# A linear-attention kernel on one core: the scores of a step made two steps ahead, its small products in two halves, and a new order

## The chip, the core and the metric

The kernel runs on one core of one Trainium2 chip. TensorE (PE) multiplies, with its weight loads overlapping the products; VectorE (DVE), ScalarE (ACT) and GpSimd (POOL) do the element work; SyncE (SP) issues nearly all loads. What is measured is the device time of one execution in microseconds.

## The reference

Attention with a decaying state feeds a gated feed-forward block. Inputs are q, k, v of shape (4, 8, 768, 64), `w_in` (512, 1024), `conv_w` (3, 1024) and `w_out` (1024, 512). Cut to what is computed:

```python
state = zeros((B, H, D, D))
for t in range(S):
    state = gamma[None, :, None, None] * state + einsum('bhd,bhe->bhde', k[:, :, t], v[:, :, t])
    y[:, :, t] = scale * einsum('bhd,bhde->bhe', q[:, :, t], state)
x = y.transpose(0, 2, 1, 3).reshape(B, S, H * D)
h = maximum(x @ w_in, 0)
conv_out[t] = conv_w[0] * h[t-1] + conv_w[1] * h[t] + conv_w[2] * h[t+1]     # per channel
out = (h * sigmoid(conv_out)) @ w_out
```

## The kernel before, in words

**Steps.** Tokens are taken in chunks of 64, for two of the four batches at a time, so there are 24 steps: 0 to 11 for the first two batches, 12 to 23 for the others. A step `n` holds all 8 heads of its chunk. The recurrence is done per chunk: scores (k times q, 64x64 for each head and batch), masked with the decay by VectorE (`masked`, L823), then multiplied with v ("within" the chunk); q times the state that earlier chunks left ("across"), where the state is copied out of PSUM by ScalarE (`carry`, L831, tile `cy`); and the update of the state in PSUM (tile `ps_st`). Steps 0 and 1 have a wider form of their own. q is scaled by VectorE first (`scale_q`, L716), v by VectorE (L722) or ScalarE (L741).

**The small products.** All of these are issued by `multiply` (L772). `mix(n)` issues those of a step, two by two in turn from two lists: 32 scores of step n+1 beside 32 "within" products of step n in records of the trace, then 32 updates of the state beside 32 "across" products. A product of the scores or of the state goes from one half of the array's rows to the same half of its columns, a product of y to the other half, so the two lists in turn use all four quarters of the array. Step 2 makes its own scores (`EARLY = 2`); a list without a partner stands alone (`mix.23` has neither next scores nor a state to update).

**The large products.** y is copied out (`y_copy`, L859, from unit 1 on) and turned into x by `x_head` (ScalarE, L909) and `x_rest`, `xt_rest` (VectorE, through `difference`, L855). Four steps make a unit, six units in all. Unit 0 multiplies x with `w_in` plainly (`mm1`, L1022, 12 records a product); units 1 to 5 by a seven-product scheme on halves and sums of the operands (`fast`, L1022, 6 records). Sums of these in SBUF (`hc`, L1054, L1049), the convolution (`conv_tap` L1089 on ScalarE, `conv_side` L1094 on VectorE), the gate (L1099, L1104) and a split of the result in two (`g_head` L1112, `g_rest` L1121) lead to the second product with `w_out` (`mm2`, L1246, 6 records; `seven` L1223 in the last unit), and `put` (L1250) copies the output to SBUF for its store.

**What sets the order.** The order on each engine is written out by hand as one string of letters per engine (`ORDER`, L80), and each engine runs its string strictly in turn. `list_tasks` (L192) names each task's dependencies; `plan` (L409) walks the strings once, at build time, and decides which of the buffers of a pool a task takes (`BUFS`: 4 `rw` buffers, one per step in flight, each holding q, k, kt and v; 7 PSUM banks `ps`; one `cy`). On the chip a task waits for its data and for the last user of its buffer. The loads stand on SyncE's queue in the order of the `DMA` string, at most 8 in flight (`fetch`, L617 to L626), so a load that waits for its buffer holds up the loads behind it.

The string of TensorE is read like this: `a` is a `mix`, `A` to `C` are `mm1` and `fast` of the units 0 and 1, `o` and `O` are `mm2` and later letters further units, `u` is `seven`. The lines that the prediction speaks of are those named above; in the changed file they stand 16 to 23 lines lower (L772 becomes L788, L823 L846, L716 L732, L855 L878, L1022 L1045, L1246 L1269).

Of the kernel before, what the change touches and what calls it, by code (L numbers as in the profile page):

```python
# [29 lines left out]
NC = S // C  # L30
# [44 lines left out]
EARLY, V_ON_ACT = 2, [*range(WIDE, 8), *range(14, N_STEPS)]  # L75
# [6 lines left out]
        "rfsfrgqssatataAAqAAAaaABBBBBaBAABBaaaooCCCIOICCCIOOICCCOIOoIoCOooCCIooIooOooOaoooaooooooooaooooooooDDDJa"  # L82
        "JDDDJPPJDDDJPPaJDPPPDDJaJoPoooaooaoooooooooEEEKoKEEEKQQKEQQQEEKaKEEEKoKQQQaooaooaooooooooFFFLoLoFFFLRRLF"
        "RRRFFLaLFFFLRoLRoRaaooooooGGGMoMoSSGGGMoMoSSoGGGMoMoSSoGGGMoMoSSuuuuuuuuuuuuuuuuuuuuuuuuuuuuuuuuuuuuuuuu"
        "uuuuuuuuuuuuuuuu"
    ),
    "DVE": (
        "kmtkqtmmmmbrbqrllb9blmlbqqlr0b9mBlr9b80mqq0ybzylzbbmdlq9ellvyqrrm332244r3m2j4r3j2j46j8ymzzb0IdCCyyObIeCC"
        "lOzzIbldCvClbqeOvyybbzzldlClyeIyzzOydmyqzzyzyedqqCmzveyyzzdvred3r322rr44e332244mjjjjqhmqvDDJPDDyyJzzPmyD"
        "zJPDyzJddeDqDyzyPzmrqerrm3d3y3224eyzz6rdj424e324mjjj8qqEiEQKEEyKQqyKzzmyyzzdEdEEeQQKreqmyEyzzmrr33y232d4"  # L90
        "y4rzz234e2jj64dj8mejhiFFhLRqFLFyyzRLzymyqzzFddReFyFyLzzmrr332244FeRrr332244djjjjiehyGGyMSzzyyzziGGdMSday"
        "eyfGzzMSGedyaeyzGzfMSGdayyzzefdaefuuuuuuuuuuuuuu"
    ),
# [60 lines left out]
def states_with(n):  # L154
    if n == NC:
        return []
    return [NC] if n == NC - 1 else [n] * (n % NC + 1 < NC)
# [251 lines left out]
def plan(tasks):  # L409
# [17 lines left out]
    def earliest(k):  # L427
# [13 lines left out]
        for name, _ in take:  # L441
            if len(slots[name]) < sum(name == x for x, _ in take):
                return None
# [920 lines left out]
```

## Time and profile before

| what | value |
|---|---|
| median of three runs | 333.06 us (331.17 to 334.36) |
| the profiled execution, its own time | 333.49 us |
| its span, first to last instruction | 331.7 us |
| PE busy | 319.0 us, 96% of the span |
| VectorE busy | 290.2 us, 88% |
| ScalarE busy | 221.6 us, 67% |
| granted TensorE clock | 1.00 throughout |
| the chain that ended last | PE 82%, DVE 6%, DMA 5%, ACT 3%, issue 2% |

A row of the timeline gives the start, the duration, the engine, the line, what is written and read, the shapes and the number of instructions put together; in brackets stands how long the engine was idle just before, and what ended that. "issue" there means a wait for nothing that the profile shows. Durations of PE overlap their neighbours a little, since matmuls are pipelined: the time that a group takes is the distance from its start to the next group's start. The span is 1.8 us shorter than the execution's own time, and the execution itself 0.43 us above the median.

### The profile page before, as it was taken

To read this page: it belongs to the slowest core of one execution; us is meant where nothing else is said; L and a number is where in the kernel's file an instruction comes from. 1 tells how busy PE (TensorE), PEld (TensorE's weight loads), DVE (VectorE), ACT (ScalarE), POOL (GpSimd) and SP (SyncE) were. 2 spreads that over 40 slices of the span, in tenths; PEclk is the share of its full clock that TensorE was granted. 3 is DMA by queue.
4 is the path that set the end of the run, shared out by engine and by line. 5 is a ranking of instruction groups with operands and counts; after the bars stand their busy time and mean duration, and the time that the engine had idled before them with its cause. 6 is when DMAs were issued, how large, how long until landed. Compare 5 with 4: busy or idle time off the path is not lost.

```text
span 331.7 us, 10665 instructions
## 1 busy us (share of the span) xinstructions
PE 319.0 (96%) x4551; PEld 286.6 (86%) x4551; DVE 290.2 (88%) x551; ACT 221.6 (67%) x447; POOL 25.8 (8%) x64
## 2 busy tenths in 40 slices
PE   7998998899999999999999999999999999999995
PEld 5787998799878888999788999888999979899994
DVE  1999899899999979679999088999789999999976
ACT  1687898886668655389867466986537773767630
POOL 2000000000101011100000100002010013001100
PEclk9999999999999999999999999999999999999999
DMA  7996954792004541522256203260001001001103
GB/s 241 388 358 219 344 182 143 243 393 98 0 3 131 158 121 73 208 81 68 94 171 214 76 21 99 78 213 0 3 33 37 2 34 63 0 3 63 65 0 128
DMA packets 21019, 40.21 MB, mean 121 GB/s; under 512 B 2742, under 2 KB 3254, under 8 KB 20972
## 3 DMA queue, kind: packets, MB, share of 16 engines
q1 hardware_dynamic: 19228, 34.15, 30.4%
q0 software_dynamic: 1600, 5.24, 4.1%
q8 instruction: 36, 0.59, 0.7%
q10 hardware_dynamic: 144, 0.13, 0.1%
q14 instruction: 11, 0.09, 0.1%
HBM read 33.23 MB, written 6.29 MB: 119 GB/s over the span
## 4 chain that ended last, share of the span: by engine, by line
PE 82%; DVE 6%; DMA 5%; ACT 3%; issue 2%; SPq 1%; DVEq 0%; ACTq 0%
PE ps L1022 35%; PE ps L1246 31%; PE ps L772 7%; PE ps L1223 6%; PE ps_st L772 4%; DMA w<-in_w_in 3%; DMA rw<-in_qk 2%; SPq L624 1%; DVE g L1121 1%; DVE hc L1054 1%; DVE t L855 1%; DVE hc L1094 1%; DVE hc L1104 1%; DVE xa L855 0%; DVE rw L823 0%
## 5 line engine op out<-in xcount | busy, mean ns | idle before, releaser
L1246 PE MATMUL ps<-w,g 128*128 128x512 f32 x480 | 118.1, 397 | 0.0
L1246 PEld LDWEIGHTS ps<-w,g 128*128 128x128 f32 x480 | 87.7, 188 | 19.0
L1022 PE MATMUL ps<-xa,w 128*128 128x256 f32 (+3 forms) x552 | 76.4, 283 | 0.5 <-DVE rw L823 0.4
L1022 PEld LDWEIGHTS ps<-xa,w 128*128 128x128 f32 x552 | 70.7, 189 | 2.6 <-ACT w L990 0.6
L1022 PE MATMUL ps<-xa,s 128*128 128x256 f32 (+2 forms) x480 | 69.3, 282 | 0.0
L1094 DVE SCALAR_TENSOR_TENSOR hc<-hc,cw_sb,hc 128x512 f32<-128x512 f32 (+1 forms) x96 | 68.1, 743 | 1.3 <-ACT hc L1089 1.2
L1022 PEld LDWEIGHTS ps<-xa,s 128*128 128x128 f32 x480 | 62.5, 189 | 1.8 <-ACT hc L1049 0.2
L1054 DVE CUSTOM_DVE_ANT_0 hc<-ps,hc 128x256 f32<-128x256 f32 (+2 forms) x80 | 32.5, 419 | 16.1 <-ACT hc L1049 10.4
L1049 ACT COPY hc<-ps 128x256 f32<-128x256 f32 (+2 forms) x60 | 22.2, 372 | 35.1 <-PE ps L1022 33.0
L1089 ACT ACTIVATE hc<-hc,cw_sb 128x512 f32<-128x512 f32 x48 | 33.5, 722 | 11.8 <-DVE hc L1054 8.5
L772 PEld LDWEIGHTS ps<-rw 64*64 64x64 f32 (+2 forms) x1472 | 27.8, 136 | 8.5 <-ACT t L859 2.1
L772 PE MATMUL ps<-rw 64*64 64x64 f32 (+2 forms) x1472 | 31.6, 223 | 2.9 <-ACT t L859 1.9
L1099 ACT ACTIVATE hc<-hc 128x1024 f32<-128x1024 f32 x24 | 25.2, 1060 | 7.9 <-DVE hc L1094 7.8
L1104 DVE TENSOR_TENSOR hc<-hc,hc 128x1024 f32<-128x1024 f32 x24 | 29.1, 1217 | 1.1 <-ACT hc L1099 1.0
L855 DVE TENSOR_TENSOR xa<-t,xa 128x384 fp32r<-128x384 f32 (+5 forms) x45 | 24.7, 567 | 3.7 <-ACT xa L909 1.2
L772 PE MATMUL ps<-rw,cy 64*64 64x64 f32 x672 | 24.3, 219 | 1.9 <-issue 1.9
L772 PE MATMUL ps_st<-rw 64*64 64x64 f32 (+1 forms) x672 | 24.4, 219 | 1.2 <-issue 1.0
L1121 DVE TENSOR_TENSOR g<-hc,g 128x1024 fp32r<-128x1024 f32 x20 | 24.4, 1220 | 1.3 <-ACT g L1112 1.3
L1112 ACT CAST g<-hc 128x1024 fp32r<-128x1024 f32 x20 | 21.0, 1049 | 5.8 <-PE ps L1246 3.7
L772 PEld LDWEIGHTS ps<-rw,cy 64*64 64x64 f32 x672 | 21.8, 135 | 2.2 <-issue 2.2
L772 PEld LDWEIGHTS ps_st<-rw 64*64 64x64 f32 (+1 forms) x672 | 22.0, 135 | 1.6 <-issue 1.2
L741 ACT ACTIVATE rw<-rw,const_sb 128x128 f32<-128x128 f32 x64 | 20.5, 395 | 0.0
(89 smaller groups left out, 356.2 us busy)
## 6 DMA issues: line engine op xcount, KB each, us to landing
rw<-in_qk SPq DMA_DIRECT2D x48, 256.0 KB, 3.6
rw<-in_kv SPq DMA_DIRECT2D x46, 256.0 KB, 4.4
out_y<-t POOLq DMA_DIRECT2D x20, 256.0 KB, 2.3
w<-in_w_in SPq DMA_DIRECT2D x16, 256.0 KB, 5.2
w<-in_w_out SPq DMA_DIRECT2D x16, 256.0 KB, 5.3
out_y<-t SPq DMA_DIRECT2D x2, 256.0 KB, 2.0
out_y<-t SPq DMA_DIRECT2D x3, 128.0 KB, 1.7
out_y<-t ACTq DMA_DIRECT2D x1, 128.0 KB, 1.8
```

Of the source, the lines that this page charges most:

```text
L772: nc.tensor.matmul(out, lhsT, rhs, start=start, stop=stop, skip_group_check=True)
L855: nc.vector.tensor_tensor(out=out, in0=in0, in1=in1, op=ALU.subtract)
L1022: nc.tensor.matmul(ps, w(a, k), x(b, k), start=first and i == 0, stop=last, skip_group_check=True)
L1049: nc.scalar.copy(quarter(u, p, *((0, 1), (0, 0), (1, 1))[i]), strip("X", u, p))
L1054: nc.vector._custom_dve(dve_ops.TENSOR_ADD_SAT, out=quarter(u, p, *out), in0=strip(bank, u, p), in1=quarter(u, p, *other), s0=float("inf") ...
L1089: nc.scalar.activation(cv, h, AF.Copy, scale=w)
L1094: nc.vector.scalar_tensor_tensor(out=cv, in0=h, scalar=w, in1=cv, op0=ALU.mult, op1=ALU.add)
L1099: nc.scalar.activation(cv, cv, AF.Sigmoid)
L1104: nc.vector.tensor_tensor(out=cv, in0=h, in1=cv, op=ALU.mult)
L1112: nc.scalar.copy(g_of(u, p)[:, 0], cv_of(u, 2 * p))
L1121: nc.vector.tensor_tensor(out=lo, in0=cv_of(u, 2 * p), in1=hi.bitcast(F32), op=ALU.subtract)
L1246: nc.tensor.matmul(ps, g, w, start=(f == 0 and i == 0), stop=(f == NF - 1 and i == 2))
```

## The change

`mix(n)` is cut in two tasks, `half(n)` and `mix(n)`. Each runs one pair of lists: the "within" products of step n beside scores, or the "across" products beside the update of the state. Normally "within" comes first; in the steps of `ACROSS_FIRST` (10, 15, 17, 19, 22) it comes second. The scores that stand beside the "within" products are those of step n+1 up to step 7, and from step 8 on those of step n+2 (`TWO_AHEAD = 8`). Step 9 lies at the border: nobody makes its scores ahead, so `scores.9` is a task of its own (`OWN`). Step 22 has no scores to stand beside its "within" products any more. `halves(n)` says what a step's halves hold:

```diff
-EARLY, V_ON_ACT = 2, [*range(WIDE, 8), *range(14, N_STEPS)]
+OWN, TWO_AHEAD, ACROSS_FIRST = (0, 1, 2, 9), 8, (10, 15, 17, 19, 22)
+V_ON_ACT = [*range(WIDE, 8), *range(14, N_STEPS)]
...
+def halves(n):
+    state = n + 1 if n == NC - 1 else n if n % NC + 1 < NC and n != NC else None
+    scored = n + 1 + (n >= TWO_AHEAD)
+    within = ("within", scored if scored < N_STEPS else None)
+    if n % NC == 0:
+        return [within]
+    return [("across", state), within] if n in ACROSS_FIRST else [within, ("across", state)]
...
+    def run_half(n, i):
+        kind, extra = halves(n)[i]
+        across, straight = list(of_y(n, kind)), []
+        if extra is not None:
+            straight = list(of_scores(extra) if kind == "within" else of_state(extra))
+        for at in range(0, len(across), 2):
+            for product in straight[at : at + 2] + across[at : at + 2]:
+                multiply(*product)
+
+    @emits
+    def half(n):
+        run_half(n, 0)
...
-        across = list(of_y(n))
-        straight = list(of_scores(n + 1)) if EARLY < n + 1 < N_STEPS else []
-        straight += [product for m in states_with(n) for product in of_state(m)]
-        for i in range(0, max(len(across), len(straight)), 2):
-            for product in straight[i : i + 2] + across[i : i + 2]:
-                multiply(*product)
+        run_half(n, len(halves(n)) - 1)
```

The dependencies in `list_tasks` follow (a `masked` after the half that made its scores, a `carry` after the "across" half), and `plan` may now give one task two banks of the same pool. All five order strings are new. The number of products is the same, and so is the number of tasks on VectorE, ScalarE, POOL and of the loads. The start of TensorE's string, where `h` is a half and `s` a `scores`:

```diff
-        "rfsfrgqssatataAAqAAAaaABBBBBaBAABBaaaooCCCIOICCCIOOICCCOIOoIoCOooCCIooIooOooOaoooaooooooooaooooooooDDDJa"
+        "rrsfsgqfsaatthqaAAAAAhaAhaABBBhaBBBBABhahaohasoCCCIOICCCIOOICCCOOIooIooCooOoooCoCIooIohaOoOhooahaooooooo"
```

Three places in the new order.

On TensorE, at the end of step 7 and the start of step 8. Before, the last "across" pairs of step 7 (`rw_3` and `cy_0` are its buffers) are followed at once by step 8, whose "within" products (into `ps_1_1146`) stand beside the scores of step 9 (`rw_1` into `ps_3_1147`):

```order
L772 MATMUL ps_st_83<-rw_3_572 64x64 x2
L772 MATMUL ps_3_1060<-rw_3_572,cy_0_1053 64x64 x2
L772 MATMUL ps_3_1147<-rw_1_882 64x64 x2
L772 MATMUL ps_1_1146<-rw_0_726 64x64 x2
L772 MATMUL ps_3_1147<-rw_1_882 64x64 x2
```

After, one large product `mm2` stands between, the scores beside step 8 (into `ps_5_1165`) are those of step 10, whose buffer `rw_2` is the one that step 6 used:

```order
L788 MATMUL ps_st_83<-rw_3_589 64x64 x2
L788 MATMUL ps_5_1062<-rw_3_589,cy_0_1099 64x64 x2
L1269 MATMUL ps_0_1146<-w_8_929,g_0_906 128x512 x3
L1269 MATMUL ps_0_1146<-w_9_934,g_0_906 128x512 x3
L788 MATMUL ps_5_1165<-rw_2_1058 64x64 x2
L788 MATMUL ps_3_1164<-rw_0_709 64x64 x2
L788 MATMUL ps_5_1165<-rw_2_1058 64x64 x2
L788 MATMUL ps_3_1164<-rw_0_709 64x64 x2
```

and behind step 8's "across" pairs (with `cy_0_1162`) come the scores of step 9, alone (`ps_6_1245`):

```order
L788 MATMUL ps_st_83<-rw_0_709 64x64 x2
L788 MATMUL ps_3_1164<-rw_0_709,cy_0_1162 64x64 x2
L788 MATMUL ps_6_1245<-rw_1_856 64x64 x16
L1269 MATMUL ps_1_1275<-w_8_929,g_0_906 128x512 x3
L1269 MATMUL ps_1_1275<-w_9_934,g_0_906 128x512 x3
```

What moved: a large product has come into the run of small ones, the scores of 10 have come up by a whole step, and the 32 scores of 9 have lost the "within" products that stood beside them.

On VectorE, at the same place. Before, the mask of step 8 (`rw_0_726`) is followed by the rest of x of the steps 4 to 7 (`xa_0_1042`), which the `fast` products of unit 1 read:

```order
L855 TENSOR_TENSOR t2_1_1058<-t2_1_1058 128x2x128
L823 TENSOR_TENSOR rw_0_726<-ps_1_1061,mask_67 128x512
L855 TENSOR_TENSOR t2_1_1058<-t2_1_1058 128x128
L855 TENSOR_TENSOR xa_0_1042<-t2_3_671,xa_0_1042 128x8x62
L855 TENSOR_TENSOR t2_1_1058<-t2_1_1058 128x128
L855 TENSOR_TENSOR xa_0_1042<-t2_2_1137,xa_0_1042 128x6x64
```

After, the scaling of q of step 10 (L732, `rw_2_1058`) stands between the mask and that rest:

```order
L878 TENSOR_TENSOR t2_1_1055<-t2_1_1055 128x128
L846 TENSOR_TENSOR rw_0_709<-ps_6_1063,mask_67 128x512
L878 TENSOR_TENSOR t2_1_1055<-t2_1_1055 128x128
L732 TENSOR_TENSOR rw_2_1058<-rw_2_1058,gq_0_1016 128x512
L878 TENSOR_TENSOR xa_0_1013<-t2_0_694,xa_0_1013 128x8x62
L878 TENSOR_TENSOR xa_0_1013<-t2_3_1155,xa_0_1013 128x6x64
L878 TENSOR_TENSOR t2_3_1155<-t2_3_1155 128x2x128
L878 TENSOR_TENSOR xa_0_1013<-t2_2_911,xa_0_1013 128x8x64
```

What moved: one 128x512 operation, which waits for the load of step 10's q, now stands ahead of the last operations on `xa`.

On VectorE and TensorE, at the steps 22 and 23. Before, the mask of step 23 (`rw_3_3441`) stands on VectorE behind convolution work (`hc`) of unit 4's products:

```order
L1054 ISA hc_5_3933<-ps_1_3926,hc_5_3933 128x256
L1094 SCALAR_TENSOR_TENSOR hc_0_3983<-hc_3_3807,cw_sb_75,hc_0_3983 128x512
L1054 ISA hc_5_3933<-ps_4_3985,hc_5_3933 128x256
L1094 SCALAR_TENSOR_TENSOR hc_0_3983<-hc_3_3807,cw_sb_75,hc_0_3983 128x512 x2
L823 TENSOR_TENSOR rw_3_3441<-ps_4_4014,mask_67 128x512
L855 TENSOR_TENSOR xa_0_4079<-t2_3_3547,xa_0_4079 128x6x62
```

After, it stands ahead of the sums of two weight tiles (`top`, of `w_12` and `w_13`), 31 places earlier:

```order
L878 TENSOR_TENSOR rw_0_3722<-top_0_68,rw_0_3722 128x256 x2
L878 TENSOR_TENSOR rw_0_3722<-top_1_69,rw_0_3722 128x256 x2
L846 TENSOR_TENSOR rw_3_3502<-ps_6_3729,mask_67 128x512
L1208 TENSOR_TENSOR top_0_68<-w_12_1496 128x256
L1209 TENSOR_TENSOR top_1_69<-w_13_1506 128x256
L878 TENSOR_TENSOR top_1_69<-top_1_69,top_0_68 128x256
```

and TensorE has these rows at the end of step 22 and in step 23 (step 22's "across" pairs with `cy_0_3912`, its "within" products alone, then step 23, whose two lists stand alone as they did before):

```order
L788 MATMUL ps_st_83<-rw_2_3348 64x64 x2
L788 MATMUL ps_1_4037<-rw_2_3348,cy_0_3912 64x64 x2
L788 MATMUL ps_1_4037<-rw_2_3348 64x64 x16
L788 MATMUL ps_0_4097<-rw_3_3502 64x64 x16
L788 MATMUL ps_0_4097<-rw_3_3502,cy_0_4092 64x64 x16
L1269 MATMUL ps_3_4139<-w_8_929,g_0_4026 128x512 x3
L1269 MATMUL ps_3_4139<-w_9_934,g_0_4026 128x512 x3
```

What moved: the scaling of q and the mask of the steps 22 and 23, four operations of VectorE, have gone to an earlier part of unit 4, and step 22's "within" products have lost the scores that stood beside them, which are made in step 21.

## Rows read from the trace of the kernel before

**Rows 1.** Windows of us: busy time (count) of each engine, PEclk, DMA share, GB/s
```profile
core 0: us, PE busy (x) PEld busy (x) DVE busy (x) ACT busy (x) POOL busy (x), PEclk, DMA share, GB/s
20.00:30.00 10.00, 9.03 (x161) 8.35 (x160) 9.93 (x20) 7.99 (x20) 0.00 (x0) 1.00 0.90 325
30.00:40.00 10.00, 8.47 (x199) 8.13 (x199) 8.58 (x17) 8.38 (x20) 0.00 (x0) 1.00 0.77 259
...
50.00:60.00 10.00, 8.13 (x342) 7.72 (x343) 9.56 (x22) 8.81 (x22) 0.00 (x0) 1.00 0.38 128
60.00:70.00 10.00, 9.68 (x137) 8.95 (x129) 9.20 (x20) 8.62 (x22) 0.61 (x3) 1.00 0.96 326
...
260.00:280.00 20.00, 19.88 (x278) 17.21 (x277) 19.55 (x43) 13.49 (x25) 3.60 (x6) 1.00 0.11 41
...
300.00:320.00 20.00, 20.00 (x160) 19.46 (x159) 19.83 (x41) 11.92 (x21) 2.34 (x4) 1.00 0.11 40
```

**Rows 2.** Timeline of PE, steps 2 to 4, 16 to 35 us
```profile
17.24 1.27 PE L772 MATMUL ps<-rw 64*64 64x64 f32 x64 [0.26 <-DMA rw<-in_qk]
...
23.24 4.48 PE L1022 MATMUL ps<-xa,w 128*128 128x256 f32 x36 [0.35 <-DVE rw L823]
...
30.34 0.21 PE L772 MATMUL ps<-rw,cy 64*64 64x64 f32 x1 [0.96 <-issue]
...
32.12 0.28 PE L772 MATMUL ps_st<-rw 64*64 64x64 f32 x2 [0.23 <-ACT cy L831]
...
33.88 0.27 PE L772 MATMUL ps<-rw,cy 64*64 64x64 f32 x2 [0.96 <-issue]
```

**Rows 3.** Timeline of PE, steps 7 and 8, 52 to 66 us
```profile
56.13 1.20 PE L772 MATMUL ps<-rw 64*64 64x64 f32 x62 [1.19 <-ACT t L859]
...
58.99 1.22 PE L772 MATMUL ps<-rw 64*64 64x64 f32 x63 [0.68 <-ACT t L859]
...
61.02 0.27 PE L772 MATMUL ps_st<-rw 64*64 64x64 f32 x1 [0.32 <-issue]
...
64.64 0.88 PE L1022 MATMUL ps<-xa,w 128*128 128x256 f32 x6
```

**Rows 4.** The chain that ended last: start, us, what
```profile
78.14 1.40 PE ps L1246 x6
79.54 0.71 PE ps L1022 x6
...
100.95 4.40 PE ps L1246 x18
```

**Rows 5.** Timeline of PE, the end of unit 1 and step 9, 90 to 100 us
```profile
98.86 1.16 PE L772 MATMUL ps<-rw 64*64 64x64 f32 x64 [0.52 <-DVE hc L1054]
```

**Rows 6.** Timeline of ACT, behind step 7, 48 to 62 us
```profile
58.36 0.59 ACT L859 COPY t<-ps 128x512 f32<-128x512 f32 x1 [0.70 <-PE ps L772]
...
59.39 0.58 ACT L831 COPY cy<-ps_st 128x512 f32<-128x512 f32 x1
```

**Rows 7.** Timeline of PE, step 23, 260 to 275 us
```profile
262.78 1.13 PE L772 MATMUL ps<-rw 64*64 64x64 f32 x32
...
264.77 8.64 PE L1246 MATMUL ps<-w,g 128*128 128x512 f32 x36
```

**Rows 8.** Timeline of DVE, 92 to 100 us
```profile
94.65 1.22 DVE L1121 TENSOR_TENSOR g<-hc,g 128x1024 fp32r<-128x1024 f32 x1
```

**Rows 9.** Timeline of PE, step 15, 160 to 168 us
```profile
165.98 0.27 PE L772 MATMUL ps_st<-rw 64*64 64x64 f32 x2 [0.66 <-issue]
```

**Rows 10.** DMA issues, part 6 of the page: count, KB each, median us to landing
```profile
rw<-in_qk SPq DMA_DIRECT2D x48, 256.0 KB, 3.6
...
w<-in_w_in SPq DMA_DIRECT2D x16, 256.0 KB, 5.2
```

**Rows 11.** Timeline of DVE, steps 22 and 23, 236 to 266 us
```profile
250.67 0.69 DVE L823 TENSOR_TENSOR rw<-ps,mask 128x512 f32<-128x512 f32 x1
...
251.94 0.68 DVE L716 TENSOR_TENSOR rw<-rw,gq 128x512 f32<-128x512 f32 x1
```

More of the change, by code (lines that the diff above doesn't have):

```diff
@@ L217, in list_tasks @@
         first, width = FIRST_STEP[u], UNITS[u]
[L218 removed]
+        wide, own = n < WIDE, n in OWN
         load(("load_q", n), 4 * P * 512, take=[("rw", n)])
@@ L249, in list_tasks @@
                 pe(("scores", n), 960, [("scale_q", n), ("load_k", n)], banks, count=32)
-            after = [("scores", n) if own else (("mix", n - 1), 0 if n - 1 == NC else -880)]
+            after = [("scores", n) if own else half_with(n - 1 - (n - 2 >= TWO_AHEAD), "within")]
             task(("masked", n, 0), DVE, tt(512), after, free=banks)
-            after = [scaled, ("masked", n, 0), ("mix", n - 1), ("load_kt", n)]
-            after += [c and (("carry", n - 1), -900), both and ("scale_q", n + 1), both and ("load_k", n + 1)]
-            count = 32 + 32 * (c > 0) + 32 * both + 32 * len(states_with(n))
-            after += [("scale_v", NC), ("load_kt", NC)] if n == NC - 1 else []
-            pe(("mix", n), 960 if n == NC else 1935, after, [y] + [("ps", ("s", n + 1))] * both, [("rw", n)] + [("cy", n - 1)] * (c > 0), count)
+            for i, (kind, extra) in enumerate(halves(n)):
+                last = i == len(halves(n)) - 1
+                after = [("half", n) if i else ("mix", n - 1)]
+                if kind == "within":
+                    after += [scaled, ("masked", n, 0)]
+                    after += [extra and ("scale_q", extra), extra and ("load_k", extra)]
+                else:
+                    after += [("carry", n - 1), extra and ("load_kt", extra), extra and (scaled if extra == n else ("scale_v", extra))]
+                take = [y] * (i == 0) + [("ps", ("s", extra))] * (kind == "within" and extra is not None)
+                free = [("rw", n)] * last + [("cy", n - 1)] * (kind == "across")
+                pe(("mix" if last else "half", n), 967, after, take, free, 32 + 32 * (extra is not None))
         if n >= WIDE - 1 and c + 1 < NC:
-            task(("carry", n), ACT, act(512, 45), [("state", n) if wide else ("mix", n - (n == NC))], [("cy", n)])
+            task(("carry", n), ACT, act(512, 45), [("state", n) if wide else half_with(n - (n == NC), "across")], [("cy", n)])
         few = TOKENS[u][0] - FIRST_STEP[u] % NC * C if n == first else 0
@@ L441, in earliest @@
         for name, _ in take:
-            if len(slots[name]) < sum(name == x for x, _ in take):
+            n = sum(name == x for x, _ in take)
+            if len(slots[name]) < n:
                 return None
-            t = max(t, min(slots[name].values()))
+            t = max(t, sorted(slots[name].values())[n - 1])
         return t
```

52 lines of the change are left out of this document (25 added, 27 removed), and 2 rows, old and new, of the table LETTER.

## Prediction

> **What bounds the kernel now.** I read the windows first. In the last stretches TensorE is busy for 19.88 of 20 us and 20.00 of 20 us, with the granted clock at 1.00, the upper of its two levels; VectorE stands at 19.55 and 19.83 [rows 1]. So TensorE sets the end, with VectorE close behind. What the change can give back is time in which TensorE stands still or goes slowly, and such time lies mostly in the first 70 us: 9.03, 8.47, 8.13 and 9.68 of 10 us [rows 1]. Then I read the timeline of TensorE there, for the waits before each group and what ended them, and the same around the steps 9, 15 and 22, where the order changes.
>
> In the opening there are two knots. At the steps 2 to 4 TensorE waits 0.26 us for a load of q, 0.35 for a mask, 0.23 for the carried state, and twice 0.96 for nothing that the profile shows ("issue") [rows 2]. At the steps 6 to 8 three steps of small products stand in a row, and step 7 and step 8 begin 1.19 and 0.68 us late, because ScalarE has first to copy y out of the bank (L859); inside step 8 there is an "issue" wait of 0.32 [rows 3].
>
> **A price to keep in mind: products without a partner.** The 64 small products of step 23 have no second list beside them and take 264.77 - 262.78 = 1.99 us [rows 7]; the 128 products of step 9 stand in pairs of lists and take 100.95 - 98.86 = 2.09 us [rows 4, 5]. That is 31 ns against 16 ns each. The reader sees here that a list that has lost its partner costs as much alone as both did together: 32 records alone cost 32 x 15 ns = 0.48 us more than in a pair. The count of products does not change, but the pairing does: the scores of 9 and the "within" products of 22 were in pairs, with each other's neighbours, and now stand alone. So the change adds 2 x 0.48 us of TensorE time. Nothing hides it.
>
> **Part by part.**
>
> Steps 3 and 4. They are pulled apart by large products, so the carry and the mask have work to hide behind: the 0.23 and the 0.35 go, -0.58 (at most this, at least nothing if the mask is late elsewhere). The two "issue" waits have no cause in the trace. What the rows show is where they stand: in the second half of a step's 128 small products, and the second one in a step that follows another at once [rows 2]; the 0.66 in step 15 stands in the second half of a step too, though nothing small stands just ahead of it [rows 9]. After the change a step still has its 128 products in one run, only two steps in a row are rarer. I take half of the second one, -0.5; the ends are 0 and -1.92.
>
> The rule that speaks here is in the Trainium skill, "Runtime: NRT & Kernel Launch", section "Instruction fetch mechanics": instructions are streamed in blocks by the engine itself, and crossing a block's border is mostly hidden. If the waits are such crossings that the denser run has laid bare, the row shows 0.96 for one that is not hidden; by the rule all of it would go once the runs are shorter, and the sum would hold -1.92 in place of -0.5. It stands below as a rival.
>
> The start. SyncE's queue has a new order, and step 2 waits 0.26 for a load of q [rows 2]. Step 2's products move up in TensorE's order by a piece. I take -0.3, with 0 and -1.0 as ends: the first loads are bound by the transfers themselves (DMA busy 0.90 in the window from 20 us on [rows 1]), and the nearest row for a bound is what TensorE idled in that window, 10 - 9.03 = 0.97 us.
>
> Steps 6 to 8. Between 56.13 and 64.64 lie 8.51 us [rows 3], in which two steps of 2.09 and two `mm2` of 1.40 are done [rows 4, 5]: 6.98, so 1.53 are lost, and 1.19 ahead of them: 2.72. After: step 7's first half still needs the bank that y of step 6 leaves, one copy of 0.59 [rows 6] and a hop behind the end of step 6, so I keep 0.65; the "across" half of step 7 needs the carry of step 6, which ScalarE makes behind that copy in 0.58 [rows 6], 0.2 to 0.3 after the first half is done: 0.3. The `mm2` between the steps 7 and 8 hides the copies of step 7. The scores of 9 alone cost 0.48, and one more turn between large and small products 0.1. Then x of unit 1 must be ready on VectorE, whose queue now has the scaling of q of step 10 ahead of it: +0.1. Together 1.63 where 2.72 were: -1.1. The ends: if neither copy is waited for, -2.0; if both old waits of 1.19 and 0.68 come back, +0.1.
>
> Unit 1. The wait of 0.52 ahead of step 9 [rows 5] goes, since step 9 moves behind the first `mm2` of unit 0's last tiles. But these read what VectorE's split (L1121) makes, which ends at 94.65 + 1.22 = 95.87 [rows 8]. TensorE now starts unit 1's products at about 64.64 - 2.5 = 62.1, and has 25 of them at 0.71 and 10 `mm2` at 1.40 ahead [rows 4]: it arrives at 62.1 + 17.7 + 14.0 = 93.8. So VectorE must be 2.1 us earlier, too. It idles 0.07 + 1.42 + 0.44 + 0.80 = 2.73 us in the windows 20 to 40 and 50 to 70 [rows 1], mostly where TensorE stands still; I take it to be 1.7 earlier and leave a wait of 0.4. That is -0.1.
>
> Step 15. Half of its 0.66 [rows 9]: -0.3 (0 to -0.66).
>
> Steps 22 and 23. Four operations of VectorE, of 0.68 and 0.69 us [rows 11], leave the stretch in which it is full and go to one where it is not. This gives no time by itself; it lets TensorE keep its lead to the end, as VectorE comes through 2.7 us earlier. The "within" products of 22 alone cost +0.48. The 1.99 of step 23 stay.
>
> The loads. From step 8 on a step's "within" half needs q and k of step n+2, whose buffer (one of four) is free only when step n-2 is done. For step 8 that leaves step 7 and one `mm2`, 2.09 + 1.40 and the 0.95 of waits: 4.4 us; a load takes 3.6 us from issue to landing [rows 10], and the scaling 0.68 [rows 11]: 4.3. It just fits. Ahead of step 11 TensorE's order has two products of unit 1, three `mm2` and step 10 (1.42 + 4.2 + 2.09 = 7.7), ahead of step 14 step 13 and seven products (2.09 + 4.97 = 7.1): room enough. I take +0.15 for all; the ends are 0 and the third rival.
>
> The sum, against the profiled execution's own 333.49 us: -0.58 - 0.5 - 0.3 - 1.1 - 0.1 - 0.3 + 0.48 + 0.15 = -2.25, so 331.2. The profiled execution is 0.43 above the median of the runs: **330.8 us**.
>
> **The rivals.**
>
> First, all "issue" waits go: 1.42 more in the steps 3 and 4 and 0.36 more in step 15, so 330.8 - 1.8 = 329.0. For it: the waits stand in dense runs only, and the runs are shorter now. Against it: step 15's stands in a step by itself [rows 9]. The page named above would have it so.
>
> Second, VectorE swallows the lead. If it is no earlier at 95.87 [rows 8] than before, TensorE waits the full 2.1 there instead of 0.4, and 330.8 + 1.7 = 332.5 is left: nothing that can be told from before. For it: VectorE is busy for 9.93 of 10 us from 20 to 30 us and 9.56 from 50 to 60 [rows 1], and its queue has got the scaling of 10 earlier. Against it: its idle time lies where TensorE stood.
>
> Third, slower: the loads made two ahead come late. In step 8 nothing is in hand, so every us that q of step 10 lands later than the row's 3.6 is a us of TensorE. From 2.2 us later on, 5.8 in all, the whole gain is gone. Loads of w took 5.2 as a median [rows 10], and 60 to 70 us is a window with the DMA at 0.96 [rows 1]. With 4 us later: 4.0 in step 8, 1.3 in step 14 and 0.7 in step 11 (what 3.6 + 4 + 0.7 has over 7.1 and 7.7, rounded), 330.8 + 6.0 = 336.8. Against it: from 50 to 60 us, when that load would run, the DMA is busy for only 0.38 [rows 1].
>
> That the change does nothing to the opening can be left out: the order there is another.
>
> **How the numbers follow.** The forecast has 0.46 (its own range is 329.5 to 332.0), the first rival 0.20, the second 0.22, the third 0.12. About 1% is what a measurement of this kernel can tell from no change: the bounds are 329.7 and 336.4. Faster are the first rival and a good quarter of the forecast, 0.20 + 0.13 = 0.33; slower three quarters of the third and a little of the second, 0.12; the rest, 0.55, is the same. The range reaches from a little under the first rival, 328.2, to 334.5, over the second with its own wait and a load wait of 2 us; it leaves out most of the third and what lies under the first.
>
> **What would show it.** The waits of 1.19 and 0.68 gone and one of about 0.65 ahead of step 7; unit 1's first product at about 62.1; a wait at the first `mm2` that reads the split of 0.4 or of 2; 32 records alone at about 1 us in the steps 9 and 22; the "issue" waits in steps 3 and 15 there or not. A wait of step 8 for the load or the scaling of step 10 would make the forecast wrong, and so would a lead at 64 us that is gone at 100.

## The result, and the profile after

The changed kernel takes **329.89 us** (median of 19 runs, 328.22 to 331.79) where the kernel before takes 333.08 (19 runs, 330.83 to 340.53): ratio 0.9908, interval 0.9885 to 0.9931. The forecast was 330.8 with 328.2 to 334.5. A ratio compares undisturbed executions only (those of the kernel before have medians of 332.6 to 333.0 us, and 334.9 beside the last experiment), so in the experiments below it can be nearer to 1 than the two medians are.

The profiled execution of the changed kernel took 331.79 us, the longest of its 19; the kernel was therefore traced a second time (`again_after`, 329.41), and so was the kernel before (`before_again`, 332.97, where the first trace was 333.49). What stands in both traces of a kernel belongs to it.

First, the page of the changed kernel (part 1), which answers to the table of before, and its windows, which answer to [rows 1]:

```profile
PE 322.2 (98%) x4551; PEld 288.2 (87%) x4551; DVE 290.1 (88%) x551; ACT 221.9 (67%) x447; POOL 27.0 (8%) x64
```

```profile
20.00:30.00 10.00, 10.00 (x195) 9.43 (x188) 9.48 (x17) 9.22 (x18) 0.00 (x0) 1.00 0.85 295
30.00:40.00 10.00, 9.76 (x218) 9.41 (x209) 9.95 (x20) 9.71 (x26) 0.06 (x1) 1.00 0.82 259
...
50.00:60.00 10.00, 9.31 (x386) 8.24 (x388) 9.96 (x24) 9.36 (x24) 0.50 (x2) 1.00 0.64 205
60.00:70.00 10.00, 9.29 (x124) 8.76 (x113) 8.80 (x20) 7.67 (x17) 0.19 (x1) 1.00 0.95 327
```

In the three windows from 20 to 40 and from 50 to 60 us TensorE is busy for 29.07 of 30 us, where it was busy for 25.63 [rows 1]. Of the 29.07, 0.88 are three products of zeros (`keep_warm`, L633, from 20.19 to the next product at 21.07), which do no work of the kernel: `plan` puts them where TensorE would otherwise wait, and the kernel before has none in these windows. The timeline of TensorE, changed kernel, first trace (start, us, engine, line, operation, count, idle before and what ended it):

```profile
20.19 0.97 PE L633 MATMUL ps<-warm 128*128 128x512 f32 x3
...
30.68 1.67 PE L1045 MATMUL ps<-xa,w 128*128 128x256 f32 x12 [0.24 <-ACT hc L1089]
...
54.12 1.15 PE L788 MATMUL ps<-rw 64*64 64x64 f32 x60 [0.53 <-ACT t L882]
55.43 0.27 PE L788 MATMUL ps_st<-rw 64*64 64x64 f32 x2 [0.16 <-ACT cy L854]
...
60.25 1.10 PE L788 MATMUL ps<-rw 64*64 64x64 f32 x32
61.28 1.66 PE L1269 MATMUL ps<-w,g 128*128 128x512 f32 x6
62.78 0.87 PE L1045 MATMUL ps<-xa,w 128*128 128x256 f32 x6
...
67.20 0.95 PE L1045 MATMUL ps<-xa,s 128*128 128x256 f32 x6 [0.71 <-ACT hc L1072]
```

The two "issue" waits of 0.96 [rows 2] and the one of 0.32 [rows 3] are gone, and where ScalarE's copies of y were waited for, 1.19 and 0.68, there is 0.53 left for y, and 0.16 for the carry. The 32 scores of step 9 alone take 61.28 - 60.25 = 1.03 us. Further on, the first two rows stand in step 14 and at the second output tile of unit 2 ([rows 9] had 0.66 in step 15), the others at the steps 22 and 23 [rows 7]:

```profile
156.52 0.27 PE L788 MATMUL ps_st<-rw 64*64 64x64 f32 x2 [0.19 <-issue]
...
160.15 5.80 PE L1269 MATMUL ps<-w,g 128*128 128x512 f32 x24 [0.47 <-DVE hc L1077]
```

```profile
260.34 2.03 PE L788 MATMUL ps<-rw 64*64 64x64 f32 x64
262.21 1.10 PE L788 MATMUL ps<-rw,cy 64*64 64x64 f32 x32
263.24 2.12 PE L1269 MATMUL ps<-w,g 128*128 128x512 f32 x8
```

The 96 records alone take 263.24 - 260.34 = 2.90 us, 30 ns each, the pace of [rows 7].

### The profile page after: what moved, and what is told of

It is laid out like the page before. It is cut to its first block, busy times and chain, and to the rows that moved or that the text cites. A ratio compares the mean times of both kernels' runs of the same rounds, so it can differ in the third digit from the quotient of the medians.

```text
span 330.1 us, 10667 instructions
## 1 busy us (share of the span) xinstructions
PE 322.2 (98%) x4551; PEld 288.2 (87%) x4551; DVE 290.1 (88%) x551; ACT 221.9 (67%) x447; POOL 27.0 (8%) x64
## 4 chain that ended last, share of the span: by engine, by line
PE 73%; DMA 9%; DVE 8%; ACT 7%; SPq 1%; issue 1%; DVEq 0%; ACTq 0%
PE ps L1045 30%; PE ps L1269 30%; PE ps L788 5%; PE ps L1246 5%; PE ps_st L788 3%; DMA rw<-in_qk 3%; DMA w<-in_w_in 2%; DMA w<-in_w_out 2%; DMA rw<-in_kv 2%; SPq L640 1%; DVE hc L1117 1%; DVE t L1260 1%; DVE hc L1077 1%; DVE hc L1127 1%; ACT top L996 1%
## 5 line engine op out<-in xcount | busy, mean ns | idle before, releaser
L1045 PE MATMUL ps<-xa,s 128*128 128x256 f32 (+2 forms) x480 | 68.6, 282 | 0.7 <-ACT hc L1072 0.7
L788 PEld LDWEIGHTS ps<-rw 64*64 64x64 f32 (+2 forms) x1472 | 29.1, 137 | 6.0 <-issue 1.4
L788 PE MATMUL ps<-rw 64*64 64x64 f32 (+2 forms) x1472 | 32.7, 225 | 0.7 <-ACT t L882 0.5
```

Of the source, the lines that this page charges most:

```text
L788: nc.tensor.matmul(out, lhsT, rhs, start=start, stop=stop, skip_group_check=True)
L1045: nc.tensor.matmul(ps, w(a, k), x(b, k), start=first and i == 0, stop=last, skip_group_check=True)
```

## The experiments

Theory A is that of the prediction: the steps pulled apart in the opening bring the gain, the lists without a partner cost about 1 us, and the order behind must let the lead through. Rival B: the scores two ahead, with the masks out of VectorE's last stretch, bring it. Theory F came with the first traces: the waits for nothing shown are fetches of instructions.

### Both kernels again

The changed kernel, unchanged:

> The changed kernel itself, once more. Its profiled execution took 331.79 us, 1.9 over its own median, so its trace may show waits that are not in most executions: 0.71 us ahead of the sixth product of unit 1, 0.47 ahead of the second tile of unit 2's first output, and products that start at 21.07 us. If these are an accident of that execution, this trace shows less of them and a span near 328; if they belong to the kernel, they stand here again. Ratio expected 0.991.

Measured: 330.07 us (median of 11, 328.98 to 332.49), ratio 0.995 (0.992 to 0.9981). TensorE's timeline:

```profile
16.75 1.27 PE L788 MATMUL ps<-rw 64*64 64x64 f32 x64 [0.89 <-DMA rw<-in_qk]
...
53.06 1.38 PE L788 MATMUL ps<-rw 64*64 64x64 f32 x64 [0.47 <-DVE rw L846]
...
157.76 5.83 PE L1269 MATMUL ps<-w,g 128*128 128x512 f32 x24 [0.48 <-DVE hc L1077]
```

The 0.71 in unit 1 is not there: it was an accident of the first execution. The 0.48 at the second output tile of unit 2 is: it belongs to the kernel. No "issue" wait is left. What stands behind the 0.48 is on VectorE:

```profile
154.09 0.69 DVE L732 TENSOR_TENSOR rw<-rw,gq 128x512 f32<-128x512 f32 x1 [1.72 <-DMA rw<-in_qk]
```

The scaling of q of step 17 waits 1.72 us for its load, which is made two steps ahead, and the gate and the sum that the tile waits for stand behind it in VectorE's order.

The kernel before, unchanged:

> The kernel before once more, for a second trace. The executions of the kernels whose opening has steps in a row (before, and two experiments) lie 6 to 10 us apart, those with other borders of the instruction blocks or with the steps apart only 2 to 4. Theory F: in these steps a late fetch of instructions costs now 1, now 3 us and some clock. Then this trace has waits for nothing shown at the records 473, 600 or 1234 again, of other lengths than 0.96, 0.96 and 0.32. If they are the same to a few hundredths, the spread comes from elsewhere.

Measured: 332.97 us, one execution. TensorE's timeline:

```profile
31.44 1.09 PE L772 MATMUL ps<-rw 64*64 64x64 f32 x58 [0.88 <-ACT rw L741]
...
60.25 0.27 PE L772 MATMUL ps_st<-rw 64*64 64x64 f32 x1 [0.47 <-issue]
...
165.50 0.27 PE L772 MATMUL ps_st<-rw 64*64 64x64 f32 x2 [0.94 <-issue]
```

The "issue" waits at TensorE's matmuls number 473 and 600 (how they are counted stands below) are missing, those at 1234 and 2633 have other lengths. Where step 3's 0.96 is missing, step 4 waits 0.88 for the scaling of v on ScalarE (L741) instead: the one had hidden the other. So of the 2.50 us that the opening lost in the steps 3 and 4 in the first trace [rows 2], 0.88 is what is left in this one.

### The opening alone, and the rest alone

The opening alone is the changed kernel's order for all tasks that ran ahead of 64.6 us, then the order of before, with one step ahead throughout:

```diff
-OWN, TWO_AHEAD, ACROSS_FIRST = (0, 1, 2, 9), 8, (10, 15, 17, 19, 22)
+OWN, TWO_AHEAD, ACROSS_FIRST = (0, 1, 2), 24, ()
```

> The order of the changed kernel up to the first product of unit 1 on every engine, with scores one step ahead throughout, and from there on the order of before. Theory A: the gain is made in the opening, by pulling the steps 3 and 4 and the steps 7 and 8 apart. Then this takes about 330.2 us: the changed kernel's gain, and 0.5 more or so, since no list of products has lost its partner. Rival B: the gain comes from the scores made two ahead and the order behind it, which lighten the end for VectorE. Then this takes 332.5 to 333.

Measured: 332.72 us (12 runs, 330.40 to 333.61), ratio 1.0003 (0.9959 to 1.0046).

```profile
68.49 0.97 PE L1018 MATMUL ps<-xa,s 128*128 128x256 f32 x6 [0.98 <-DVE hc L1050]
...
98.19 1.16 PE L761 MATMUL ps<-rw 64*64 64x64 f32 x64 [0.52 <-DVE hc L1050]
```

In the steps 3 to 8 the opening has 0.24 and 0.23 us of waits left (and 1.67 ahead of step 2), and still the executions together show no gain (the interval leaves room for 0.4%). The 0.98 us that go to VectorE right behind the opening are new; the 0.52 stood there before too [rows 5]. That is the second rival's mechanism, in its place: with the old order behind it, VectorE takes back a part of the lead. How much of it is not shown: this execution of 331.91 us is itself 1.1 and 1.6 us shorter than the two traces of the kernel before, and it has no "issue" wait.

The rest alone has the order of before up to there (with the loads, the factors and the scaling of step 10 brought forward, and `scores.9`), then the changed kernel's:

> The order of before up to the first product of unit 1 (with the loads, the scaling of q and the factors of step 10 brought forward, which the scores two ahead need, and the scores of 9 alone), and from there on the changed kernel. Theory A: two lists alone cost 0.96, nothing else is won but half of step 15's wait, so about 333.6. Rival B: 330 to 331.

Measured: 334.76 us (12 runs, 331.36 to 337.52), ratio 1.0002 (0.9948 to 1.0057).

```profile
31.10 1.09 PE L761 MATMUL ps<-rw 64*64 64x64 f32 x58 [0.89 <-ACT rw L730]
...
56.31 1.09 PE L761 MATMUL ps<-rw 64*64 64x64 f32 x58 [1.79 <-ACT t L855]
59.15 1.22 PE L761 MATMUL ps<-rw 64*64 64x64 f32 x62 [0.76 <-PE ps L761]
```

The old waits of the opening are here, 3.44 us in these three rows; this execution is the second shortest of the 12. Neither half shows a gain by itself, both together do: the first run came out where B expected it, the second nearer to A's number than to B's. In all of these kernels other products stand at the borders of the instruction blocks (the last section of the experiments), so the halves do not differ in the order alone.

### One step ahead in the new order

```diff
-OWN, TWO_AHEAD = (0, 1, 2, 9), 8
+OWN, TWO_AHEAD = (0, 1, 2), 24
```

and every mask of the steps 9 to 23 at the earliest place on VectorE that its scores allow.

> The changed kernel with the scores one step ahead throughout: no scores alone in step 9, step 22's "within" products in a pair again, and each mask of the steps 9 to 23 on VectorE as early as its scores allow; all else in the order of the changed kernel. Theory A: two lists in pairs again give back 0.96, but a mask (0.69) and its way stand between the steps that follow each other at once (10 and 11, 12 and 13, 15 and 16, 19 and 20, 22 and 23), about 1 us each where nothing hides it: 331 to 335. Rival: the masks are hidden, and one step ahead is as good: 329.

Measured: 333.35 us (12 runs, 331.56 to 334.24), ratio 0.9991 (0.9957 to 1.0025).

```profile
111.88 1.09 PE L761 MATMUL ps<-rw 64*64 64x64 f32 x58 [0.83 <-DVE rw L819]
...
149.77 1.09 PE L761 MATMUL ps<-rw 64*64 64x64 f32 x58 [0.68 <-DVE rw L819]
...
263.24 1.15 PE L761 MATMUL ps<-rw 64*64 64x64 f32 x32 [1.00 <-DVE rw L819]
```

Three masks are waited for, ahead of the steps 11, 13 and 23: 2.51 us, and 0.9 comes back from the pairs. The 333.35 against 330.07 (ratios of 0.9991 against 0.995 and 0.9908) is what the scores two ahead are worth in this order. The three waits less the pairs are 1.6 us of it; they show that the scores two ahead take the mask off the way where a step follows another at once. The rest has not been located. The prediction had not priced that, since in the order of before those steps stood apart.

### The price of a list alone

The order of before, with one step ahead and "within" first throughout as in the opening alone, and with eleven pairs of lists taken apart (cut):

```diff
+OWN = (0, 1, 2, *range(13, 24))
-    within = ("within", scored if scored < N_STEPS else None)
+    within = ("within", scored if scored < N_STEPS and scored not in OWN else None)
```

> The order of before, but the scores of the steps 13 to 23 are made by themselves, right behind the "within" products of the step ahead, beside which they stood in turn: the same products, 11 pairs of lists taken apart. Theory: 64 records in a pair take 0.96 us and 64 records alone 1.99 us (step 23), about 0.95 more for each of the 11 pairs, so TensorE's busy time rises by about 10 us and the time to 341 to 343. Rival: step 23's slow pace is its own (its operands come from the mask just before), and nothing changes: 333.

Measured: 344.09 us (4 runs, 340.44 to 346.13), ratio 1.0356 (1.028 to 1.0433). Step 13, "within" and scores one behind the other, up to the first row of the state:

```profile
146.24 1.85 PE L761 MATMUL ps<-rw 64*64 64x64 f32 x62
147.88 0.27 PE L761 MATMUL ps<-rw,cy 64*64 64x64 f32 x2
```

About 64 records in 1.64 us, 26 ns each, against 16 in pairs [rows 4, 5]: the price is there. The trace is of the shortest of the four executions, 340.44 - 333.49 = 7.0 us longer than the trace before, 0.63 per pair; the ratio of 1.0356 stands for some 12 us, 1.1 per pair (0.85 to 1.3). Step 23's 0.95 lies between the two.

### The order of the halves

```diff
-ACROSS_FIRST = (10, 15, 17, 19, 22)
+ACROSS_FIRST = ()
```

> The changed kernel with the "within" products first in every step, also in the steps 10, 15, 17, 19 and 22; the order strings as they are. What is undone is the early carry of these five steps, and the later need of their mask and of the loads two ahead. Theory A: nothing in these steps is on the path but step 15 and 16, so 330 to 330.5. Rival: the carry of a step that is followed at once by another (10, 15, 19, 22) is waited for, 0.6 and a hop each: 332 to 333.

Measured: 338.54 us (6 runs, 335.43 to 342.98), ratio 1.0157 (1.0095 to 1.0219). The trace is of the longest of them, so its lengths are an upper end. Timeline of TensorE, the chain, and the windows behind (columns as in [rows 1]):

```profile
102.24 0.98 PE L1018 MATMUL ps<-xa,w 128*128 128x256 f32 x6
...
108.41 2.10 PE L761 MATMUL ps<-rw 64*64 64x64 f32 x64 [3.07 <-DMA rw<-in_qk]
```

```profile
102.75 5.52 DMA rw<-in_qk
```

```profile
108.40:112.00 3.60, 3.60 (x68) 3.19 (x69) 2.33 (x5) 0.00 (x0) 0.00 (x0) 0.50 0.06 20
```

Both expectations missed it. Step 10's "within" half needs q and k of step 12, whose buffer step 8 had left long before: q was issued at 69.27 us. But on SyncE's queue the four loads stand as q of 12, q of 13, k of 12, k of 13 (`qqkk` in the `DMA` string), and q of 13 waits for the buffer of step 9. Step 9 ends at about 102.3 us, q of 13 is issued at 102.37, k of 12 behind it at 102.75, and it lands 5.52 us later: TensorE stands 3.07 us, and behind that the granted clock is 0.50, the lower of its two levels. (Two waits for ScalarE follow, 1.25 and 2.12 us at 117.48 and 123.28.) The third rival's mechanism, a load for two steps ahead that comes late, is real, in step 10 rather than step 8, and by the order of the queue rather than by the length of the load; the "across" half put first covers it. Whether k of 12 ahead of q of 13 on the queue would do the same was not run. With step 10 alone turned:

```diff
-ACROSS_FIRST = (10, 15, 17, 19, 22)
+ACROSS_FIRST = (10,)
```

> The changed kernel with the "across" products first in step 10 alone, no longer in 15, 17, 19 and 22. With none of the five, step 10's first half stood 3.07 us for the load of q of step 12, whose buffer step 8 leaves, and the clock fell behind it. Theory L: it is step 10 alone in which the order of the halves covers a load; then this takes 330 to 330.7. Rival: the early carries of the steps 15, 19 and 22, which are followed at once by another step, count too: 331 to 333.

Measured: 331.08 us (12 runs, 329.79 to 333.10), ratio 0.9957 (0.9921 to 0.9993): most of the way back. Between this and the changed kernel's 330.07 and 329.89 no difference is shown, though this trace has three waits, 0.28, 0.56 and 0.31 us from 198 us on, that neither trace of the changed kernel has. So the expectation's load was the wrong one of the two (k, not q), and its step the right one.

### Steps in a row again

The changed kernel with two products moved on TensorE:

```diff
- half.3 mix.3 mm1.0.5.0 half.4 mix.4 ... mix.7 mm2.0.0.0 half.8 mix.8 scores.9
+ half.3 mix.3 half.4 mix.4 mm1.0.5.0 ... mix.7 half.8 mix.8 scores.9 mm2.0.0.0
```

> The changed kernel with two large products moved on TensorE alone: the one between the steps 3 and 4 goes behind step 4, the one between the steps 7 and 8 goes behind the scores of 9, so that the steps stand in a row again. Theory A: the carry of step 3 is waited for again (0.2), and y of step 7 and the carry of 7 ahead of step 8 (0.65 to 1), and one wait without a shown cause of up to 0.96 comes back in step 4: 330.9 to 331.9. Rival: the waits of before came from other parts of the order (VectorE, ScalarE), and it stays at 330.

Measured: 336.78 us (6 runs, 332.51 to 337.94), ratio 1.0126 (1.0038 to 1.0213), far above both expectations. The timeline, and two windows:

```profile
30.85 1.37 PE L761 MATMUL ps<-rw 64*64 64x64 f32 x62 [1.24 <-DVE rw L705]
...
57.83 1.22 PE L761 MATMUL ps<-rw 64*64 64x64 f32 x62 [0.95 <-DVE rw L705]
...
62.45 0.37 PE L761 MATMUL ps_st<-rw 64*64 64x64 f32 x2 [2.99 <-issue]
...
162.36 0.27 PE L761 MATMUL ps_st<-rw 64*64 64x64 f32 x2 [1.42 <-issue]
```

```profile
59.40:62.40 3.00, 0.05 (x3) 0.00 (x0) 1.42 (x4) 0.83 (x3) 0.00 (x0) 0.99 0.98 313
62.40:65.40 3.00, 2.95 (x71) 2.84 (x70) 0.66 (x5) 1.52 (x5) 0.00 (x0) 0.50 0.93 322
```

The scaling of q of the steps 5 and 10 on VectorE (L705), which had cover while the steps stood apart, is now waited for: 2.19 us in the first two rows. And an "issue" wait of 2.99 us has come into step 8, with the clock at 0.50 behind it. The one execution of the six with a mean granted clock of 1.00 took 332.51 us, the others, at 0.992 to 0.995, 336.07 to 337.94. So most of what lies above the expectations seems to go with this wait and the clock behind it, and less with the order of the steps as such; only one of the six was traced.

### What the "issue" waits are

Counting TensorE's matmuls from the start of the trace up to such a wait gives its record. Windows of the kernel before, from 0 to just ahead of each wait (the count is the x of PE):

```profile
0.00:30.30 30.30, 26.70 (x473) 21.61 (x474) 21.82 (x39) 18.30 (x40) 2.45 (x12) 1.00 0.90 319
0.00:33.80 33.80, 29.05 (x600) 23.68 (x600) 24.93 (x47) 21.02 (x44) 2.45 (x12) 1.00 0.86 302
0.00:61.00 61.00, 54.00 (x1234) 47.81 (x1234) 50.59 (x94) 46.15 (x103) 3.03 (x14) 1.00 0.75 260
0.00:165.90 165.90, 157.78 (x2633) 140.21 (x2634) 145.19 (x257) 119.73 (x243) 11.21 (x36) 1.00 0.52 177
```

600 - 473 = 127, 1234 - 600 = 634 = 5 x 126.8, 2633 - 1234 = 1399 = 11 x 127.2: whole multiples. In the kernel with the steps in a row again the wait of 2.99 us stands at record 1232; in the changed kernel the 0.19 of step 14 stands at 2505, one block short of 2633. And each of these waits ends 1.4 to 1.5 us behind the end of a packet of the instruction queue, of 16 KB: in the kernel before packets end at 28.83, 32.48, 59.61 and 164.54, the waits at 30.34, 33.88, 61.02 and 165.98.

The same numbers stand in the text of both kernels. `plan` counts TensorE's records, and its constant `FETCH = (61.0, 126.6, 127.3)` holds the first border and the distances between borders, the last one from record 1200 on. With the 32 records of the warming products at the start, which it does not count, this gives borders at 472.8, 599.4, 1232.4 and 2632.7: the four waits.

To test it, 32 small products, 64 records in the trace, were put at the very start of the kernel before, where TensorE waits anyway:

```diff
-    for i in range(WARM_SMALL):
+    for i in [*range(14), *range(14), *range(14), *range(4)]:
```

> The kernel before with 64 more of the small warming products at the very start, where TensorE waits for its first data; nothing else. In the traces so far every wait for nothing shown stands at a record of TensorE (473, 600, 1234 and 2633 of the kernel before, 1232 and 2505 elsewhere) that is a whole number of 126.8 records from the others, and ends 1.4 to 1.5 us behind the end of a 16 KB packet of the instruction queue. Theory F: these are fetches of instructions that come late in a run of small products. Then the waits stand at the same numbers of records again, but 64 records earlier in the program: the one in step 3 falls into its first half, behind few small products, and goes or is under 0.3, while others may come where a border now falls into the second half of a step. Rival: the waits belong to these products (a bank, a semaphore): then they stand at the same products, 64 records later in number, 0.96 each.

Measured: 333.07 us (10 runs, 332.45 to 334.99), ratio 1.0013 (0.9978 to 1.0048).

```profile
21.07 0.27 PE L772 MATMUL ps<-rw,cy 64*64 64x64 f32 x2 [0.60 <-issue]
...
60.49 0.74 PE L772 MATMUL ps<-rw 64*64 64x64 f32 x35 [0.38 <-issue]
...
150.25 1.49 PE L1022 MATMUL ps<-xa,w 128*128 128x254 f32 x10 [0.40 <-issue]
...
264.83 0.91 PE L772 MATMUL ps<-rw,cy 64*64 64x64 f32 x22 [0.45 <-issue]
```

The waits stand at the records 347, 1234, 2381 and 4161: on the old grid within a dozen records, and at other products. None is left in step 3 or 15. Then the scaling of q of step 17 and a load of step 2's time were moved in the changed kernel:

```diff
- load_w.2.0 ... load_k.3                scale_q.17 gated.2.1 sum.2.3.0 ... sum.2.3.2
+ load_k.3 load_w.2.0                    gated.2.1 sum.2.3.0 ... sum.2.3.2 scale_q.17
```

> The changed kernel with two moves: the scaling of q of step 17 on VectorE goes behind the last sum of unit 2's fourth pair of column blocks (in two traces VectorE stood up to 1.7 us for that load, made two steps ahead, and the sum that a product of w_out waited for, 0.47 and 0.48 us, stood behind it), and k of step 3 is loaded ahead of the first half of the third piece of w_in (step 2 waited 0.89 and more for it). Theory: the 0.48 goes, and some 0.3 of the start: 329.3, and no wait of TensorE at the second output tile of unit 2. Rival: another wait takes their place behind, and the time stays at 330.

Measured: 330.07 us (12 runs, 328.56 to 332.50), ratio 0.9916 (0.9877 to 0.9955): no gain over the changed kernel is shown.

```profile
156.65 0.27 PE L761 MATMUL ps_st<-rw 64*64 64x64 f32 x2 [1.45 <-issue]
```

The wait of 0.48 is gone from the trace, as expected; in this execution record 2505 has a wait of 1.45 in its place, which was 0.19 and nothing in the two traces of the changed kernel, and step 15 waits 0.37 for the carry of step 14, which it did in neither. Last, 42 such records (21 products) at the start of this kernel:

```diff
-    for i in range(WARM_SMALL):
+    for i in [*range(14), *range(14), *range(7)]:
```

> The kernel of the two moves with 42 more of the small warming products at the very start, so that every border of the instruction blocks falls 42 records earlier in the program. In the kernel of the two moves TensorE stood 1.45 us for nothing shown at record 2505, in step 14's second half; with the borders moved that record lies 42 products later in the program, in the large products behind step 14. Theory F: no such wait in step 14, and the first tiles of w_out's products follow at once; the executions lie within 3 us of each other, median 329 to 329.8. Rival: the wait belongs to step 14's products and stays, or another border takes its place, and the median stays at 330.

Measured: 339.81 us (6 runs, 338.02 to 341.32), ratio 1.0186 (1.0112 to 1.026). Both expectations missed the time, by far. The rival's mechanism is what came: other borders take the place of the one in step 14.

```profile
22.23 0.33 PE L761 MATMUL ps<-rw,cy 64*64 64x64 f32 x4 [2.88 <-issue]
...
47.33 0.21 PE L761 MATMUL ps_st<-rw 64*64 64x64 f32 x1 [1.25 <-issue]
...
60.96 0.40 PE L761 MATMUL ps<-rw 64*64 64x64 f32 x12 [0.76 <-issue]
...
70.47 0.62 PE L1018 MATMUL ps<-xa,w 128*128 128x256 f32 x3 [1.37 <-issue]
...
119.88 0.21 PE L761 MATMUL ps<-rw,cy 64*64 64x64 f32 x1 [1.10 <-issue]
...
157.78 0.27 PE L761 MATMUL ps_st<-rw 64*64 64x64 f32 x2 [1.03 <-issue]
```

Six waits, 8.39 us, at the records 346, 852, 1106, 1360, 1996 and 2378, against a time 9.7 us longer; behind the first of them the granted clock is at 0.67 and 0.63 in the windows 22.20 to 24 and 24 to 27 us. Step 14's wait went from record 2505, but one has come into step 13, and five others elsewhere. Nothing of the work or its order behind the start was touched.

## Why the prediction was right, and where it was not

The direction, the range and the size hold: 330.8 forecast, 329.89 measured, -2.25 us against its own trace where the medians differ by 3.2 and the two pairs of traces by 1.70 and 3.56. But the sum is right with terms that are not all right.

| step of the prediction | forecast | first traces | second traces |
|---|---|---|---|
| products of zeros behind step 2 | none | +0.88 | +0.81 |
| steps 3 and 4, waits | -1.08 | 0.24 for 2.50: -2.26 | 0.24 for 0.88: -0.64 |
| start of step 2 | -0.3 | 17.24 to 17.59: +0.35 | 17.85 to 16.75: -1.10 |
| steps 6 to 8, waits (forecast 2.72 to 1.05) | -1.67 | 0.69 for 2.19: -1.50 | 0.63 for 2.34: -1.71 |
| step 9 alone, and a turn | +0.58 | +1.03 | about the same |
| end of unit 1 | -0.1 | -0.52 (and the accident, +0.71) | -0.52 |
| steps 14 and 15 and the loads | -0.15 | -0.66 + 0.19 + 0.47: 0 | -0.94 + 0.48: -0.46 |
| steps 22 and 23 | +0.48 | 3.89 for 3.99: -0.1 | as the first |

The table adds to -1.4 for the first traces, where -1.70 was measured, and to -2.7 for the second, where it was -3.56 (from 332.97 to 329.41). Of the rest 0.23 is a wait of the kernel before for VectorE at 209 us, which both its traces have and the changed kernel's do not; the remainder has not been located.

**Products without a partner.** The price holds: alone they take 30 ns each in step 22 and 23, and 1.03 us for step 9's 32. The sum of both places was forecast as 0.96 and measured as 0.93. The place was wrong: I charged 0.48 in each. In fact the opening pays the whole 1.03, since step 8 keeps its pairs with the scores of 10 on top; and the end pays nothing, since the scores that left step 22 took their own time with them.

**Steps 6 to 8.** Right in size, and in kind in the first trace: 0.53 and 0.16 where 0.65 and 0.3 were forecast, the first for ScalarE's copy of y, the second for the carry. In the second trace 0.47 stands in the place of the 0.53, and what ended it is VectorE's mask. The 2.72 that the forecast counts as lost is not all waits: the trace before has 1.19 + 0.68 + 0.32 = 2.19, and the other 0.53 lies in steps and products that took longer than the 2.09 and 1.40 taken from elsewhere. The load for step 8 did just fit, as worked out; no wait for it stands there in either trace.

**Unit 1.** The step that failed is the 0.4 at the split: there is no wait there in either trace, VectorE was as early as TensorE needed. Only in the opening alone, with the old order behind it, does VectorE take the lead back, at other places (0.98 anew, beside the 0.52 of before).

**The "issue" waits.** The step that failed most is "I take half of the second one, -0.5". The steps in the row were weighed by where in a step a wait stands; what the runs show is that a wait stands where a block of instructions ends and the next one has come late. The prediction found "no cause in the trace" and left the borders to a rival; their places stood in the kernel, in `FETCH`. In the changed kernel 0.19 and nothing are left where 2.90 and 1.41 stood in the two traces of before. So what the first rival forecast came about in the trace, but its price did not: not all of it was to be had, since the 0.96 in step 3 had covered 0.88 of another wait.

This limits what is shown of the whole change. The "issue" waits make 2.71 and 1.41 us of the differences between the pairs of traces, 1.70 and 3.56, and they depend on the borders as much as on the order: with 42 records at the start, the changed order with the two moves goes from a ratio of 0.9916 to 1.0186. The gain of 0.5% to 0.9% is measured with the borders where they are; how much of it would be left with the borders elsewhere is not shown. Nor is it shown whether they lie well by luck or because the order was chosen with `FETCH` in view.

**Loads two ahead.** The step that failed is "whose buffer (one of four) is free only when step n-2 is done", taken as the time at which a load starts. It leaves out the queue: k of step 12 stands behind q of 13, which waits for step 9. Between the end of step 9 and the first half of step 10 TensorE has 3.1 us of work, two products of unit 1 and one `mm2`, and the load takes 0.4 us to its issue and 5.5 to its landing. The prediction priced the steps 8, 11 and 14 and not step 10, and did not see what `ACROSS_FIRST` is for. The third rival is off in the changed kernel only because step 10 runs its halves the other way round. (By its own figures the rival's 1.3 and 0.7 are 1.2 and 0.6, what 8.3 has over 7.1 and 7.7.) What is left of late loads in the changed kernel is VectorE's 1.72, which costs TensorE 0.48.

**What two ahead is worth.** Not priced at all: 333.35 without it, 330.07 with it, with 2.51 of masks waited for.

What stays open: why a packet of instructions starts when it does. The packet of the border at record 2505 ended 1.35 us before TensorE came there in the first trace of the changed kernel, 1.81 in the second, and 0.11 with the two moves; the waits are 0.19, nothing and 1.45. So the difference between executions is the packet's, which started 2.32, 1.64 and 3.43 us behind the border before it. Both kernels at the same several places of the borders, which would tell the gain of the order from that of the borders, were not run. No trace shows the kernel before at the upper end of its range.

## What to carry to other kernels

A wait for nothing shown, in a run of very short instructions, is worth counting: if the records at such waits lie a fixed number apart and each ends a fixed time behind a packet of the instruction queue, it is the fetch, and moving the borders by a few dozen instructions at the start is a cheap test. Compare two orders only with that in mind: a change of order also moves which instructions lie at a border, here worth up to 8.4 us, more than the change itself. A load that is due early can be late because of the load ahead of it on the queue, and not because of its own buffer. And a lead won early in a kernel has to be let through by the order of every engine behind it: the opening alone and the rest alone showed no gain, both together 0.5% and 0.9% in the two measurements.

## What the runs showed of the hardware

Instructions of TensorE came in blocks of 16 KB, 36 packets in every trace, one for about 127 matmuls with their weight loads. The 14 traces hold 490 borders between two such blocks (places by `FETCH`, times from the packed traces). TensorE waited at 22 of them, for 0.19 to 2.99 us. At these the packet's end lay at most 1.35 us ahead of TensorE's arrival, or, twice, behind it, and TensorE went on 1.2 to 1.6 us behind the packet's end; at 453 of the other 468 borders the packet had ended 1.35 us or more ahead. A packet ahead of a wait took 0.9 to 1.4 us. In 12 of the waits it had started 0.7 to 1.3 us behind the border before, and TensorE was through with the block in 2.0 to 3.4 us; in the other 10, the waits of 2.99 and 2.88 us among them, it had started only 2.0 to 4.1 us behind that border.

All 22 waits stand behind blocks with 101 or more small products; 150 borders behind such blocks and all 318 behind others had none. The Trainium skill, "Runtime: NRT & Kernel Launch", section "Instruction fetch mechanics", calls the crossing of a block's border mostly hidden; over the 490 borders the traces agree, and behind blocks of small products 22 of 172 were not hidden.

After TensorE had stood for 2.99 us the granted clock was 0.50, the lower level of the two, in the 3 us that followed, and the same in the 3.6 us after the 3.07 us in step 10: a long wait cost more than its length.
